# Giving out the frames of a ring in falling order of their last write

## The chip, the cores and the metric

The kernel runs on one core of one Trainium2 chip. Its time is the device time of one execution in microseconds: 972.9 us as the median of three runs (972.48 to 973.26) before the change. Five engines work side by side, each on its own queue in program order: TensorE (PE, matmuls; its weight loads are shown apart as PEld), ScalarE (ACT, activation functions), VectorE (DVE), GpSimd (POOL) and SyncE (SP, which here issues transfers). They wait for each other through semaphores.

## The reference

Attention over pooled keys, and after it a two-layer network, on 4 batches of 12,288 tokens with 128 channels:

```python
kv_pool = kv.reshape(B, H // r, r, W // r, r, C).mean(axis=(2, 4))   # r = 4
k = v = kv_pool.reshape(B, -1, C) @ w_sr                             # 768 keys a batch
a = softmax(q @ k.T / sqrt(C))
x = (a @ v).reshape(B * S, D)                                        # 49,152 tokens
h = x @ w_in                                                         # 128 -> 2048
out = (h * sigmoid(1.702 * h)) @ w_out                               # 2048 -> 128
```

## The kernel before, in words

**Tiling.** Tokens go in 96 groups of 512 (`G`, `NG`). A *chunk* is 128 x 512 values after an activation function: for attention, the exponentials of the scores of one group against 128 of the 768 keys (six chunks a group, `JC`); for the network ("MoE" in the names), the gated values of one group in 128 of the 2,048 hidden channels (16 chunks a group, `FCH`). The work goes in two rounds (`R`): attention of half of the tokens, then the network of that half, and the same again.

**Steps.** `seq` lists 700 units of up to three chunks (`K`). `fill(p)` puts up the matmuls of unit p into three PSUM banks, banks 0 to 2 and 3 to 5 in turn (`fill_attn`, L329, and `fill_moe`, L508), and one activation that turns the three banks into three chunks of bf16 in `ag` (Exp at L331, the sigmoid form of Gelu at L510). I number fills and activations from 0. A *drain* is what PE does with finished chunks: `drain_attn` multiplies 128-token pieces of attention chunks with the values (18 matmuls of 129 columns for three tiles, L340), `drain_moe` multiplies one chunk with the second weights and adds up in a bank (one matmul of 512 columns, L515). VectorE takes the sums out of banks 6 and 7 (L349 and L357 for attention, L523 for the network).

**The ring.** `ag` has 102 places for chunks (`AG`). `slot_of` holds which place each living chunk has, and a drain that used a chunk for the last time takes it out. `place` gives a unit of fill its places: the chunks of the first eight groups lie at fixed places, all others at `head`, which runs through the places in turn and begins again at `low`. `room_ahead` counts the free places from `head` on, up to the first that is taken.

**Early weights.** Four groups of the second round (`early`) have their exponentials made by VectorE during the first round's network, from a score matmul of one chunk (`early_fill`, L377; the polynomial in `early_exp`). They lie in the first 24 places: at group 12 of the network, `background_moe` sets `low` to 24, so that the ring shrinks to 78 places, and the planner sets it back to 0 when the drains of `todo_early` are done.

**The planner.** The order of all engines is written out by the program itself, while it is built, with no scheduler behind it. The loop at the end goes over the units: after `fill(n + 2)` it gives out drains and extra work (transposes, keys and values of later batches, early scores) for as long as, by the planner's own costs, the next fill is still in time for ACT (`limit`). The room in the ring enters there: extra work is put off when `room` is under four units, and a drain is given out even past the limit when `room` is under 2 K + 1, or under 4 K and the drain could start at once. What changes `room_ahead` therefore can change the order on PE and, through it, on VectorE.

**Waits.** The framework adds the semaphore waits from what each instruction reads and writes. An activation waits for PE (its fill), and, where its places were written by an earlier activation, for ACT's own semaphore too, unless ACT has already waited for that value or a later one. An instruction holds one wait; a second is an instruction of its own (EVENT_SEMAPHORE) ahead of it on the queue. In the program before, 654 such instructions stand on ACT's queue.

Of the kernel before, what the change touches and what calls it, by code (L numbers as in the profile page):

```python
# [24 lines left out]
def kernel(  # L25
# [8 lines left out]
    JC = J // 128  # L34
# [3 lines left out]
    G = 512  # L38
# [5 lines left out]
    K = 3  # L44
    T = 128
# [15 lines left out]
    EARLY = 4  # L61
    AG = 102
# [29 lines left out]
    def next_acc():  # L92
        return min((m for m in (13 - last_acc, last_acc) if m not in closes), key=lambda m: free[m])
# [67 lines left out]
    def add_kv(b, n):  # L161
        i, w = divmod(n, r)
        if n == 0:
            kv_sums[b] = kvsum.tile([Hp, 2, Wp, C], F32, name="kvs")
        for i2 in range(2):
            nc.gpsimd.dma_start(out=kv_sums[b][:, i2], in_=kv_p[b, i, w, :, i2],  # L166
                                **({"accum_op": ADD} if n else {}))
# [109 lines left out]
    ag = agpool.tile([128, AG, 512], BF, name="ag")  # L277
# [11 lines left out]


    slot_of = {}
    head, low = 8 * JC, 0

    def place(chunks):
        nonlocal head
        if chunks[0][0] == "a" and chunks[0][1] < 8:

            lo = [i * JC + jc for _, i, jc in chunks]
            slot_of.update(zip(chunks, lo))
            return ag[:, lo[0]:lo[-1] + 1:JC, :]  # L300
        if head + len(chunks) > AG:
            head = low
        lo = head
        head += len(chunks)
        busy = set(slot_of.values())
        for c in chunks:
            assert lo not in busy
            slot_of[c] = lo
            lo += 1
        return ag[:, head - len(chunks):head, :]  # L310

    def room_ahead():
        busy = set(slot_of.values())
        return next((n for n in range(AG - low) if (head - low + n) % (AG - low) + low in busy), AG - low)

    early = range(NG // R, NG // R + EARLY)

# [123 lines left out]
    def gate():  # L441

        nc.vector.memset(gate_tile, 0.0)  # L443
        nc.gpsimd.memset(gate_tile, 0.0)  # L444
# [3 lines left out]
    def background(i):  # L448

        s = i // 4  # L450
        if i % 4 == 0:
            if QS <= s + 2 < NS:
                load_qT(s + 2)
            if CAST <= s + CAST < NS:
                gate()
                cast_q(s + CAST)
        if i == 10:
            gate()
            for jc in range(JC):
                load_chunk(1, jc)  # L460
        if 0 <= i - 16 < JC:
            extras.append((key_and_value, 1, i - 16))
        if 0 <= i - 15 < JC:
            extras.append((pool_chunk, 1, i - 15))
        if i == 26:
            gate()
            nc.gpsimd.dma_start(out=w_in_sb, in_=moe_w_in)
        if i == 34:
            gate()
            nc.gpsimd.dma_start(out=w_out_sb, in_=moe_w_out.rearrange("(o p) c -> p o c", p=128))  # L470

    def background_moe(g):

        n, g = divmod(g, 4 * XS)
        m, odd = divmod(g - 9, 2)
        if n == 0 and 0 <= m < (RT - LATER[0]) // PART:
            (bring_back if odd else put_away)(n, m)
        g += n * 4 * XS
        nonlocal head, low
        if g == 12:  # L480
            low = EARLY * JC
            head = max(head, low)
        if g in (40, 46):
            i = early[0] + 4 * (g // 46)
            begun.add(("a", i))
            background(i)
        for b, lo in ((2, 2), (3, 24)):
            if lo <= g < lo + 8:
                gate()
                add_kv(b, g - lo)  # L490
            if g in (lo + 10, lo + 12):
                use_kv(b, (g - lo - 10) // 2)

    def use_kv(b, a):
        nonlocal extra_at
        sum_kv(b, a)
        on_dve(3.5)
        extra_at = max(extra_at, dve + 1.5)
        extras.extend([(transpose_pooled, b, a), (make_k, b, a), (make_v, b, a)])
# [31 lines left out]
    chunks, sizes = [], [1, 3, 3, 1, 3, 1, 3, 1] + [3, 3, 2] * 4  # L531
# [5 lines left out]
    todo_early = [("a", t, a) for t in range(NT) for a in range(2) if (t // TS * TS + TS - 1) // 4 in early]  # L537
# [68 lines left out]
    PAUSE = 4.0  # L606
    now, end, extra_at = 0.0, [], 0.0
    source, dve = None, 0.0

    def on_dve(cost):  # L610
        nonlocal dve
        dve = max(dve, now + 1.0) + cost


    def fill(p):
        nonlocal now
        if p >= len(seq):
            return
        kind, part = seq[p]
        prepare(p)  # L620
        lo = K * (p % 2)
        (fill_attn if kind == "a" else fill_moe)(part, banks[:, lo:lo + len(part), :])
        if p >= 2:
            now = max(now, end[p - 2] + HANDOVER / 2)
        now += len(part)
        begin = max(now + HANDOVER / 2, end[p - 1] if p else 0.0)
        if p and kind != seq[p - 1][0]:
            begin += SWITCH
        end.append(begin + FIXED + CHUNK * len(part))
# [3 lines left out]
    for n in range(len(seq)):  # L633
        fill(n + 2)
        while True:
            room = room_ahead()
            limit = end[-1] - K - HANDOVER if n + 3 < len(seq) else 1e9
            bank = free[next_acc()]
            f = None
            if turns and max(now, bank) >= turns[0][0]:  # L640
                f, args = turn, turns[0][1:]
            if f is None and extras and now >= max(extra_at, bank):
                f, *args = extras[0]
            if steps and dve <= now + 2.0:
                early_step()
            if not f and not steps and early_todo and low and min(slot_of.values()) >= low and (2, 1) in vs and dve <= now + 2.0 and now >= bank:
                f, args = early_fill, early_todo[0]
            if f and max(now, bank) + COST[f][0] > limit + (LATE if f is turn else 0.0 if f is early_fill else 4.5) and room >= 4 * K:
                f = None
            if f:  # L650
                now = max(now, bank) + COST[f][0]
                f(*args)
                free[last_acc] = dve + 1.0 if f is early_fill else now + COST[f][1]
                if f in (transpose_pooled, make_k, make_v):
                    on_dve(2.5)
                extra_at = max(now + PAUSE, dve + 1.5 if f in (transpose_pooled, make_k, make_v) else 0.0)
                if f is turn:
                    turns.pop(0)
                elif f is early_fill:
                    pass  # L660
                else:
                    extras.pop(0)
                continue
            if not source:

                if todo_early and all((i, jc) in made for t in range(todo_early[0][1], todo_early[0][1] + TS)
                                      for i in [t // 4] for jc in range(JC)):
                    source = todo_early
                else:
                    source = todo  # L670
            if not source:
                break
            kind, i, c = source[0]
            needs = at[("at" if kind == "a" else kind, i, c)]
            cost = K * SMALL if kind == "a" else 1.0
            first_of = c == 0 and (kind == "m" or i % TS == 0)
            if source is not todo_early and (needs > n or (kind == "a" and first_of and at["at", i + TS - 1, 1] > n)
                                             or (kind == "a" and i // 4 in early and (i // 4, JC - 1) not in made)):
                if first_of:
                    source = None  # L680
                break
            start = now if source is todo_early else max(now, end[needs] + HANDOVER)
            if first_of:
                start = max(start, bank)
            if start + cost > limit and not (room < 2 * K + 1 or (room < 4 * K and start == now)):
                if first_of:
                    source = None
                break
            now = start + cost
            (drain_attn if kind == "a" else drain_moe)(i, c)  # L690
            source.pop(0)
            if not todo_early:
                low = 0
            if c == (1 if kind == "a" else FCH - 1) and (kind == "m" or i % TS == TS - 1):
                source = None
    assert not todo and not todo_early and not turns and not extras and not early_todo
# [30 lines left out]
```

## Time and profile before

| | before |
|---|---|
| time | 972.9 us (972.48 to 973.26) |
| span of the profiled run | 971.3 us |
| PE busy | 946.9 us (97%), 6,245 matmuls recorded |
| ACT busy | 946.5 us (97%), 705 instructions |
| DVE busy | 345.0 us (36%) |
| PE weight loads busy | 505.1 us (52%) |
| TensorE clock | 0.999 of full speed |

How to read it: the first round's attention runs to about 150 us, its network to 499 us, the second attention to 619 us, and the second network to the end. PE and ACT are both busy nearly all of the time, so the busy shares can't tell which of them the other waits for; a matmul's record reaches to the modelled end of its pass through the array, and so overlaps the next one's. The start-to-start time of neighbours tells more: 216 ns for matmuls of 512 columns, 57 ns for those of 129, and from end to end 1,343 ns for activations of 1,536 values that follow each other without a wait.

### The profile page before, as it was taken

How to read it: one execution, taken by the hardware profiler on the slowest of the kernel's cores; microseconds unless marked ns; L12 is line 12 of the kernel's file. 1: busy time of each engine (PE TensorE's matmuls, PEld its weight loads, DVE VectorE, ACT ScalarE, POOL GpSimd, SP SyncE). 2: the span in 40 equal slices, each digit the busy share in tenths (PEclk: the TensorE clock that was granted, in tenths of full speed). 3: DMA queues.
4: the chain of work that ended last, by engine and by line, in shares of the span. 5: the costliest groups of instructions: out<-in, count | busy, mean ns of one | idle time of the engine just before them, and what ended most of it. 6: DMA issues, size and time to landing. Idle time of an engine off the chain costs nothing.

```text
span 971.3 us, 15718 instructions
## 1 busy us (share of the span) xinstructions
PE 946.9 (97%) x6245; PEld 505.1 (52%) x6359; DVE 345.0 (36%) x734; ACT 946.5 (97%) x705; POOL 65.6 (7%) x113
## 2 busy tenths in 40 slices
PE   7899999999999999999999999999999999999997
PEld 3567777544444444454445777754444444444443
DVE  4444433201578787877312333311101101001010
ACT  4999999999999999999999999999999999999997
POOL 3100100340000232000000000000000000000000
PEclk9999999999999999999999999999999999999999
DMA  9898751899862799224338985652222222222222
GB/s 180 159 198 156 104 101 34 104 148 163 169 133 33 106 148 115 40 36 79 59 62 159 170 160 121 132 120 44 34 44 43 34 44 33 43 34 40 37 33 44
DMA packets 354169, 89.70 MB, mean 92 GB/s; under 512 B 328048, under 2 KB 351728, under 8 KB 353776
## 3 DMA queue, kind: packets, MB, share of 16 engines
q1 hardware_dynamic: 323936, 56.06, 33.3%
q0 software_dynamic: 29104, 32.51, 22.2%
q8 instruction: 49, 0.80, 0.3%
q10 hardware_dynamic: 1056, 0.13, 0.1%
q14 instruction: 24, 0.20, 0.1%
HBM read 52.49 MB, written 45.88 MB: 101 GB/s over the span
## 4 chain that ended last, share of the span: by engine, by line
PE 73%; ACT 20%; DMA 3%; issue 2%; DVE 1%; POOL 0%; POOLq 0%
PE banks L508 24%; PE banks L515 24%; ACT ag L510 19%; PE banks L340 13%; PE banks L329 10%; DMA qT<-q_bf 2%; ACT ag L331 1%; DMA x<-in_q_dram 1%; DVE qT L230 1%; PE banks L377 0%; PE banks L419 0%; PE banks L224 0%; DVE o_sb L523 0%; PE banks L134 0%; PE banks L177 0%
## 5 line engine op out<-in xcount | busy, mean ns | idle before, releaser
L510 ACT ACTIVATE ag<-banks 128x1536 bf16<-128x1536 f32 x512 | 690.1, 1534 | 2.2 <-PE banks L508 2.2
L508 PE MATMUL banks<-x,w_in_sb 128*128 128x512 bf16 x1507 | 412.8, 378 | 2.1
L515 PE MATMUL banks<-ag,w_out_sb 128*128 128x512 bf16 x1496 | 407.2, 379 | 2.5 <-ACT ag L510 0.5
L331 ACT ACTIVATE ag<-banks 128x1536 bf16<-128x1536 f32 (+1 forms) x188 | 250.7, 1446 | 13.2 <-PE banks L329 12.5
L515 PEld LDWEIGHTS <-w_out_sb 128*128 128x128 bf16 x1536 | 149.8, 98 | 181.9 <-issue 1.5
L508 PEld LDWEIGHTS <-w_in_sb 128*128 128x128 bf16 x1536 | 147.7, 97 | 177.3 <-issue 23.6
L523 DVE STREAM_TRANSPOSE o_sb<-banks 128x512 f32<-128x512 f32 x96 | 68.7, 716 | 401.8 <-PE banks L515 382.0
L340 PEld LDWEIGHTS <-ag 128*128 128x128 bf16 x2304 | 146.3, 98 | 45.0 <-issue 1.2
L340 PE MATMUL banks<-v,ag 128*128 128x129 bf16 x2304 | 162.5, 220 | 0.4 <-DVE v L158 0.3
L329 PE MATMUL banks<-qT,kT 128*128 128x512 bf16 x507 | 147.2, 379 | 9.7 <-ACT ag L331 4.8
L349 DVE RECIPROCAL rec<-banks 128x3 f32<-128x3 f32 x128 | 23.1, 180 | 132.5 <-PE banks L340 132.5
L404 DVE SCALAR_TENSOR_TENSOR ea<-ea,eb 128x512 f32<-128x512 f32 x96 | 66.1, 688 | 2.8
L329 PEld LDWEIGHTS <-kT 128*128 128x128 bf16 x552 | 47.4, 98 | 36.2 <-issue 4.5
L357 DVE TENSOR_TENSOR x<-banks,rec 128x384 bf16<-128x384 f32 x104 | 58.0, 558 | 3.6
L166 POOL DMA_DIRECT2D kvs<-in_kv_dram x32 | 40.3, 1309 | 15.7 <-DMA kvs<-in_kv_dram 11.9
L444 POOL MEMSET gate_tile<- 1x8 f32 x38 | 4.0, 106 | 462.1 <-DVE gate_tile L443 462.1
L393 DVE TENSOR_SCALAR ea<-banks 128x512 f32<-128x512 f32 x24 | 16.6, 692 | 28.0 <-PE banks L377 28.0
L406 DVE SCALAR_TENSOR_TENSOR ag<-ea,ee 128x512 bf16<-128x512 f32 x24 | 16.5, 690 | 1.2
L399 DVE SCALAR_TENSOR_TENSOR eb<-eb,ea 128x512 f32<-128x512 f32 x24 | 16.5, 689 | 0.7
L357 DVE TENSOR_TENSOR xt<-banks,rec 128x384 bf16<-128x384 f32 x24 | 13.4, 558 | 0.8
L230 DVE COPY qT<-banks 128x512 bf16<-128x512 bf16 x15 | 9.8, 687 | 5.3 <-PE banks L224 5.2
L401 DVE TENSOR_SCALAR ea<-eb 128x512 f32<-128x512 f32 x24 | 11.0, 456 | 0.7
(65 smaller groups left out, 150.8 us busy)
## 6 DMA issues: line engine op xcount, KB each, us to landing
out_dram<-o_sb SPq DMA_DIRECT2D x382, 64.0 KB, 2.0
kvs<-in_kv_dram POOLq DMA_DIRECT2D x32, 384.0 KB, 6.4
q_bf<-in_q_dram POOLq DMA_DIRECT2D x20, 512.0 KB, 7.8
x_bf<-x SPq DMA_DIRECT2D x13, 768.0 KB, 5.7
x<-in_kv_dram POOLq DMA_DIRECT2D x12, 512.0 KB, 12.7
x<-in_q_dram POOLq DMA_DIRECT2D x3, 512.0 KB, 20.0
w_in_sb<-in_moe_w_in_dram POOLq DMA_DIRECT2D x1, 512.0 KB, 5.2
w_out_sb<-in_moe_w_out_dram POOLq DMA_DIRECT2D x1, 512.0 KB, 7.0
```

Source lines behind the costliest of these rows:

```text
L166: nc.gpsimd.dma_start(out=kv_sums[b][:, i2], in_=kv_p[b, i, w, :, i2], **({"accum_op": ADD} if n else {}))
L230: nc.vector.tensor_copy(dst, src)
L329: nc.tensor.matmul(ps[:, k, :], kTs[i // GB][:, jc * 128:(jc + 1) * 128], rhs, start=True, stop=True)
L331: nc.scalar.activation(place([("a",) + c for c in chunks]), ps, AF.Exp, scale=scale)
L340: nc.tensor.matmul(av_of[u][:, k * (C + 1):(k + 1) * (C + 1)], weights(("a", i, jc))[:, o:o + T], vs[i // GB][:, jc, 0:C + 1], start=(jc = ...
L349: nc.vector.reciprocal(rec, ps[:, :, C])
L357: nc.vector.tensor_tensor(to, ps[:, :, 0:C], rec.unsqueeze(2).broadcast_to([128, TS, C]), MUL)
L404: nc.vector.scalar_tensor_tensor(a, a, COEFFS[k], b, ADD, MUL)
L508: nc.tensor.matmul(ps[:, k, :], w_in_sb[:, fc * 128:(fc + 1) * 128], x[:, g % (4 * XS) * G:(g % (4 * XS) + 1) * G], start=True, stop=True)
L510: nc.scalar.activation(place([("m",) + c for c in chunks]), ps, AF.Gelu_apprx_sigmoid)
L515: nc.tensor.matmul(o_of[g], w_out_sb[:, fc, :], weights(("m", g, fc)), start=(fc == 0), stop=(fc == FCH - 1))
L523: nc.vector.transpose(o_sb, o_of.pop(g))
```

## The change

The 102 places become 34 frames of three. `place` gives each unit one whole frame (the fixed places of the first eight groups stay). When its list `order` is empty, it takes all frames free at that time, sorted by the number of the unit that wrote them last, and gives them out from the youngest write to the oldest; then it makes a new list. `room_ahead` counts three places for every free frame, wherever it lies. The first 24 places are taken out of the list at group 12 as before, and come back when the last drain of the early groups themselves is given out (`early_left`), no longer when `todo_early` is empty.

It is meant for ACT's queue: once ACT has waited for the youngest write of a list, the other frames of the list need no wait on its own semaphore any more.

```diff
     slot_of = {}
-    head, low = 8 * JC, 0
+    low = 0
+    written = [0] * (AG // K)
+    order, unit = [], 0
+
+    def free_frames():
+        busy = {s // K for s in slot_of.values()}
+        return [f for f in range(low // K, AG // K) if f not in busy]
 
     def place(chunks):
-        nonlocal head
+        nonlocal order, unit
+        unit += 1
         if chunks[0][0] == "a" and chunks[0][1] < 8:
             lo = [i * JC + jc for _, i, jc in chunks]
-            slot_of.update(zip(chunks, lo))
-            return ag[:, lo[0]:lo[-1] + 1:JC, :]
-        if head + len(chunks) > AG:
-            head = low
-        lo = head
-        head += len(chunks)
...
+            step = JC
+        else:
+            if not order:
+                order = sorted(free_frames(), key=lambda f: written[f])
+            f = order.pop()
+            lo = range(f * K, f * K + len(chunks))
+            step = 1
+        for c, s in zip(chunks, lo):
+            assert s not in slot_of.values()
+            slot_of[c] = s
+            written[s // K] = unit
+        return ag[:, lo[0]:lo[-1] + 1:step, :]
 
     def room_ahead():
-        busy = set(slot_of.values())
-        return next((n for n in range(AG - low) if (head - low + n) % (AG - low) + low in busy), AG - low)
+        return K * len(free_frames())
...
         if g == 12:
             low = EARLY * JC
-            head = max(head, low)
+            order[:] = [f for f in order if f >= low // K]
...
+    early_left = 2 * (G // T) * EARLY
...
-            if not todo_early:
-                low = 0
+            if kind == "a" and i // 4 in early:
+                early_left -= 1
+                if not early_left:
+                    low = 0
```

More of the change, by code (lines that the diff above doesn't have):

```diff
@@ L291 @@
     slot_of = {}
-    head, low = 8 * JC, 0
+    low = 0
[4 more added lines that the diff above has]
+        return [f for f in range(low // K, AG // K) if f not in busy]
     def place(chunks):
-        nonlocal head
+        nonlocal order, unit
+        unit += 1
         if chunks[0][0] == "a" and chunks[0][1] < 8:
             lo = [i * JC + jc for _, i, jc in chunks]
-            slot_of.update(zip(chunks, lo))
-            return ag[:, lo[0]:lo[-1] + 1:JC, :]
-        if head + len(chunks) > AG:
-            head = low
-        lo = head
-        head += len(chunks)
-        busy = set(slot_of.values())
[L306 to L310, printed above, removed]
+            step = JC
[10 more added lines that the diff above has]
+        return ag[:, lo[0]:lo[-1] + 1:step, :]
     def room_ahead():
-        busy = set(slot_of.values())
-        return next((n for n in range(AG - low) if (head - low + n) % (AG - low) + low in busy), AG - low)
+        return K * len(free_frames())
     early = range(NG // R, NG // R + EARLY)
@@ L478, in background_moe @@
         g += n * 4 * XS
-        nonlocal head, low
+        nonlocal low
         if g == 12:
             low = EARLY * JC
-            head = max(head, low)
+            order[:] = [f for f in order if f >= low // K]
         if g in (40, 46):
```

## The prediction

> **What bounds the kernel now.** I read the page's chain and costliest groups first, then the chain for stretches of the span, then the waits of TensorE's weight loads, then single hand-offs in the timeline.
>
> The page says that ACT and PE are both 97% busy; the chain says which of them gates.
>
> ```profile
> PE 73%; ACT 20%; DMA 3%; issue 2%; DVE 1%; POOL 0%; POOLq 0%
> ...
> L510 ACT ACTIVATE ag<-banks 128x1536 bf16<-128x1536 f32 x512 | 690.1, 1534 | 2.2 <-PE banks L508 2.2
> ...
> L331 ACT ACTIVATE ag<-banks 128x1536 bf16<-128x1536 f32 (+1 forms) x188 | 250.7, 1446 | 13.2 <-PE banks L329 12.5
> ```
>
> Each of the 700 activations is one step: PE fills three banks, ACT turns them into one frame of the ring, PE drains older frames. Cut at 800 us, the chain is first PE's and then ACT's (two answers, 600 to 800 us and 800 to 965 us):
>
> ```profile
> by line: PE banks L508 43.3%; PE banks L515 42.1%; PE banks L340 9.9%; PE banks L329 4.1%; issue 0.6%
> ```
> ```profile
> by line: ACT ag L510 94.0%; issue 4.6%; PE banks L515 0.9%; PE banks L508 0.8%
> ```
>
> Who waits shows in the second weight load of a fill: it sits idle where PE has to wait until ACT has left the banks (total us, times, longest; 375 to 480 us, then 800 to 965 us). There are no such waits from 90 to 150 or from 480 to 800 us.
>
> ```profile
> PEld L508 <- issue: 2.1, 11, 0.2
> ```
> ```profile
> PEld L508 <- issue: 20.2, 119, 0.2
> ```
>
> So from 100 to 800 us PE runs without a break but for 22 places, where its matmuls slip 1.73 us in all by start times; only from 803 us on does it wait 52 ns in every step. In those last 165 us ACT ends one activation every 1343 ns whatever its waits.
>
> The instruction whose number the change cuts is the extra wait on ACT's queue (lines L331 and L510):
>
> ```profile
> L331 ACTq EVENT_SEMAPHORE  x138: 17/17/17, 63.6 to 617.8; - x138
> ```
> ```profile
> L510 ACTq EVENT_SEMAPHORE  x512: 17/17/17, 149.7 to 963.6; - x171
> ```
>
> Its price at a hand-off where ACT is starved: with one wait, and with two.
>
> ```profile
> 79.57 0.81 PE L329 MATMUL banks<-qT,kT 128*128 128x512 bf16 x3
> ```
> ```profile
> 80.42 1.45 ACT L331 ACTIVATE ag<-banks 128x1536 bf16<-128x1536 f32 x1
> ```
> ```profile
> 417.79 2.20 PE L340 MATMUL banks<-v,ag 128*128 128x129 bf16 x36
> ...
> 419.83 0.81 PE L508 MATMUL banks<-x,w_in_sb 128*128 128x512 bf16 x2
> ...
> 420.47 1.46 PE L515 MATMUL banks<-ag,w_out_sb 128*128 128x512 bf16 x6
> ...
> 420.73 1.45 ACT L510 ACTIVATE ag<-banks 128x1536 bf16<-128x1536 f32 x1 [1.24 <-PE banks L508]
> ...
> 422.68 1.45 ACT L510 ACTIVATE ag<-banks 128x1536 bf16<-128x1536 f32 x1 [0.49 <-PE banks L508]
> ```
>
> The first fill ends at 80.38 and ACT starts at 80.42: 36 ns in the trace's nanoseconds, at every starved start with one wait. The second ends at 420.64, ACT starts at 420.73: 97 ns. The second wait costs 61 ns, and only there. The same lines show the kernel's largest stall: 36 attention drains in one step, then six MoE drains in the next.
>
> **What the Trainium skill says.** "Perfetto Trace Analysis", Identifying Dependency Chains: an instruction that waits on several engines may have EventSemaphore instructions put before it; the 650 rows above agree. It gives no price, so I use 61 ns. "TensorE: Matmul & The Clock Gate", Back-to-back issue gap: N/2.4 + 2.5 ns, so 216 ns for 512 columns and 56 for 129; the trace has 216 and 57. "ScalarE: Activation LUTs", What ACT_TABLE_LOAD costs: 186 ns + 0.833 ns per element with immediates, neighbours overlapping by 93, so 1466 and 1373 ns; the trace has 1450 and 1343, which I use.
>
> **The change part by part.**
>
> *Extra waits: 650 down to about 70 (the built program's order).* A frame taken from the top of the falling list carries the youngest write of the list, so the wait for it covers the rest of the list. Where ACT is fed in time, the extra wait is processed while the previous activation runs, and its removal is worth nothing: that covers the 119 steps after 803 us. Where ACT is starved, PE has no break, and an activation that starts 61 ns earlier does not move the next matmul. It pays once where a PE-bound stretch passes into one in which PE waits for ACT: there PE's wait of about 52 to 60 ns shrinks. Six such stretches follow a starved start (at 88, 310, 387, 427, 462 and 803 us): at most 6 x 61 = 0.37 us, at least none. The writes are safe as before: an activation waits for its fill, which stands on PE behind all drains that freed the frame, so no new wait on PE arises. The self-waits left are for activations at least three back, long ended.
>
> *Order of PE.* Room is now counted in whole free frames. The counts of matmuls do not change; their places do: PE's order is the same through the first 177 fills (255 us), and then drains move by one step here and there. I price a step as 3 x 0.216 for its fill, 0.216 per MoE drain or early score, 0.0567 per attention drain (36 in 2.04 us), less 1.343: what is over is taken from PE's lead, what is left ACT loses. Three MoE drains give -0.05, four +0.17. The largest lead follows from before's step 335 (18 attention and 2 MoE drains, +0.76): 0.547 us were lost at 471.7, behind steps of +0.17, -0.05, -0.05, so the lead can be 0.76 + 0.07 - 0.55 = 0.28; with one wait less, 0.34.
> - Before, fills 298 to 305: 36 attention drains (+1.34), six MoE drains (+0.60), a five-drain step: ACT lost 0.12 + 1.34 + 0.60 + 0.10 = 2.17 us.
> - After, the same stretch: three drains each at 298 and 299; the 36 stand as 18 + one early score at step 303 (+0.54) and 18 + five MoE drains at 304 (+1.40). Lead before it: 0.34, less 0.17 of a four-drain step, plus 0.05 twice at most = 0.20. Lost: 0.34 + 1.40 = 1.74. Gain 0.43.
> - Step 335: before 0.55 lost; after, three MoE drains there: 0. Gain 0.54. The moved 18 come as 12 and 6 + three MoE drains at steps 345 and 346 behind two four-drain steps: lead 0.14 against +0.29, so 0.15 lost.
> - Steps 177 to 297: early scores and two groups of attention drains change places. The same walk gives 0.13 lost, less 0.11 from the hand-offs = 0.02 lost net. From 350 on, equal work in other steps: 0.01 gained.
> - Fill 54 (87.6 us) and the first PE-bound stretch: 0.05 + 0.06 gained.
>
> Sum: 0.43 + 0.54 - 0.15 - 0.02 + 0.01 + 0.11 = 0.92 us. The same walk over before's order gives each of its five large losses within 20 ns and the end within 0.5 us, and of the sum 0.3 us is the wait and 0.6 the order. 972.9 - 0.9 = 972.0.
>
> *What the trace of before does not show:* whether the moved early scores (L377) wait for VectorE to free a bank. Before, one of 24 waited, 165 ns; behind it on PE stand the next drains and fills. From below 0, from above 24 x 0.165 = 4.0 us; I take none, as VectorE is 36% busy. The changed time at which the 24 frames of early weights come back (before about fill 348, now about 356) is nothing: the walk has it in the order. Python's bookkeeping runs at build time.
>
> **The rivals.**
> - *Every starved hand-off pays.* 30 starts with two waits lost over 50 ns between 87 and 800 us: 30 x 61 = 1.8 us, and 0.6 of order: 970.5. For it: ACT is visibly idle there. Against: PE is unbroken around nearly all of them, so its work, not the hand-off, sets the pace.
> - *The order gives nothing.* PE's work is the same in sum, and the losses only change places: 0.3 of waits alone: 972.6. For it: the clump of 36 stays. Against: step 335's loss has no equal later.
> - *Slower.* The moved early scores and the 36 drains, now beside an early score, find banks that VectorE has not freed: half the bound is 2.0 us: 972.0 + 2.0 = 974.0. For it: no view of before can exclude it. Against: 23 of 24 did not wait.
>
> **How the numbers follow.** Forecast 0.62, every hand-off 0.11, order gives nothing 0.20, slower 0.07. The time is the forecast's, 972.0. The range 971.2 to 973.2 holds the first and third, with the 0.4 us by which the runs of before lie apart from their median; it leaves out the second and most of the fourth. Faster by over 0.2% is below 970.95: the 0.11. Slower by over 0.2% is above 974.85: the upper part of the fourth, 0.04. Even removing all of PE's 1.73 us of waits and the hand-off at 803 us would only reach 971.1. Within: 0.85.
>
> **What would show it.** Right: about 70 extra waits on ACT's queue; starved starts 36 ns behind the fill; ACT still one per 1343 ns after 800 us; the idle before L510 at 415 to 423 us replaced by one of about 1.7 us near 425 us; none at 471. Wrong: a DVE releaser before L377 or L340; a PE that waits in every step well before 800 us (ACT would gate more than I think); activations that last longer than 1343 ns from end to end.

## The result, and the profile after

| | before | after |
|---|---|---|
| time, first comparison | 972.69 us (972.24 to 973.26) | 971.51 us (971.32 to 972.16) |
| ratio, 95% interval | | 0.9989 (0.9971 to 1.0006) |
| the same kernel in a later comparison | 972.57 us | 971.55 us, ratio 0.9991 (0.9983 to 0.9999) |
| span of the profiled run | 971.3 us | 969.7 us |

The change gains about 1 us, 0.1%; the first comparison alone does not tell it from none, the second just does. The forecast was 0.9 us. Neither interval tells this from the rival "the order gives nothing" (0.3 us, a ratio of 0.9997); the count below does.

The page's chain and costliest groups of the kernel after:

```profile
ACT 48%; PE 47%; DMA 3%; DVE 1%; issue 1%; POOL 0%; POOLq 0%
...
L515 ACT ACTIVATE ag<-banks 128x1536 bf16<-128x1536 f32 x512 | 690.0, 1543 | 1.6 <-PE banks L513 1.5
...
L336 ACT ACTIVATE ag<-banks 128x1536 bf16<-128x1536 f32 (+1 forms) x188 | 250.6, 1445 | 12.2 <-PE banks L334 11.7
```

The activations are as busy as before to 0.2 us, and less idle in both groups (lines L336 and L515 here are L331 and L510 of the kernel before). The chain looks like another kernel's, ACT 48% where it was 20%; the experiments show that this is not to be believed. The extra waits on ACT's queue went from 650 rows to 66:

```profile
L336 ACTq EVENT_SEMAPHORE  x16: 17/17/17, 63.1 to 613.4; - x16
```
```profile
L515 ACTq EVENT_SEMAPHORE  x50: 17/17/17, 148.9 to 932.5; - x50
```

The timeline where the prediction put the remaining clump (start us, us, instruction):

```profile
423.43 0.84 PE L345 MATMUL banks<-v,ag 128*128 128x129 bf16 x12
...
424.11 0.38 PE L382 MATMUL banks<-qT,kT 128*128 128x512 bf16 x1
...
424.32 0.50 PE L345 MATMUL banks<-v,ag 128*128 128x129 bf16 x6
...
424.66 0.81 PE L513 MATMUL banks<-x,w_in_sb 128*128 128x512 bf16 x2
...
425.31 1.18 PE L345 MATMUL banks<-v,ag 128*128 128x129 bf16 x18
...
425.51 1.45 ACT L515 ACTIVATE ag<-banks 128x1536 bf16<-128x1536 f32 x1 [0.23 <-PE banks L513]
...
426.33 1.24 PE L520 MATMUL banks<-ag,w_out_sb 128*128 128x512 bf16 x5
...
427.41 0.81 PE L513 MATMUL banks<-x,w_in_sb 128*128 128x512 bf16 x3
...
428.25 4.15 ACT L515 ACTIVATE ag<-banks 128x1536 bf16<-128x1536 f32 x3 [1.30 <-PE banks L513]
```

18 drains and a score delay the fill at 424.66, 18 and five the one at 427.41. The first of these fills ends at 425.47, and ACT starts 36 ns later. Counted from end to end of neighbouring activations, with 1,343 ns taken off, ACT lost 0.34 and 1.40 us here and 0.17 near 485 us; the walk of the prediction (its sum over TensorE's order, step by step) had 0.34, 1.40 and 0.15.

This count is the measure of the rest of the document. It takes the time from the end of one activation to the end of the next, less the 1,343 ns of an activation that follows without a wait; what is over is what ACT *lost* there. The table sums it, in us, by number of the activation, the three loads of function tables (1.42 us each) left out. The first 52 activations lose between 9.4 and 10.6 us, differently from run to run of one kernel too; most of the difference lies at the second activation, which waits for the first inputs. So the medians scatter by half a microsecond where this count does not. Each ratio is to the runs of before in the same comparison.

| kernel | 52-179 | 180-297 | 298-356 | 357-444 | 445-699 | sum | against before | median, us | ratio to before (95%) |
|---|---|---|---|---|---|---|---|---|---|
| before | 1.36 | 0.22 | 2.73 | 1.01 | 0.81 | 6.13 | | 972.5 | |
| after | 1.27 | 0.26 | 1.93 | 0.91 | 0.91 | 5.28 | -0.85 | 971.51 | 0.9989 (0.9971 to 1.0006) |
| e1 | 1.27 | 0.16 | 2.65 | 0.93 | 0.87 | 5.88 | -0.25 | 972.20 | 0.9998 (0.9990 to 1.0006) |
| e2 | 1.31 | 0.36 | 2.05 | 0.88 | 1.12 | 5.72 | -0.41 | 972.13 | 0.9996 (0.9988 to 1.0004) |
| e3 | 1.27 | 0.26 | 1.93 | 0.00 | 0.00 | 3.46 | -2.67 | 969.81 | 0.9972 (0.9960 to 0.9983) |
| e4 | 1.27 | 0.39 | 0.44 | 5.44 | 1.15 | 8.69 | +2.56 | 975.07 | 1.0033 (1.0021 to 1.0046) |
| e5 | 1.27 | 0.16 | 2.65 | 0.93 | 0.85 | 5.86 | -0.27 | 972.05 | 0.9995 (0.9987 to 1.0004) |
| e6 | 1.27 | 0.39 | 0.44 | 0.89 | 1.15 | 4.14 | -1.99 | 970.56 | 0.9981 (0.9974 to 0.9987) |
| e7 | 1.27 | 0.39 | 0.44 | 0.00 | 0.00 | 2.10 | -4.03 | 969.17 | 0.9967 (0.9955 to 0.9980) |
| e8 | 1.27 | 0.44 | 0.97 | 0.00 | 0.00 | 2.68 | -3.45 | 969.23 | 0.9969 (0.9957 to 0.9982) |
| e9 | 1.31 | 0.50 | 1.03 | 0.12 | 0.23 | 3.19 | -2.94 | 969.43 | 0.9969 (0.9957 to 0.9981) |
| e10 | 0.46 | 0.81 | 2.33 | 0.18 | 0.00 | 3.78 | -2.35 | 970.18 | 0.9976 (0.9968 to 0.9984) |
| e11 | 1.27 | 0.26 | 1.93 | 0.91 | 0.91 | 5.28 | -0.85 | 971.55 | 0.9991 (0.9983 to 0.9999) |

### The profile page after: what moved, and what is told of

Same layout as the page of the kernel before. It is cut to its first block, busy times and chain, and to the rows that moved or that the text cites. A ratio compares the mean times of both kernels' runs of the same rounds, so it can differ in the third digit from the quotient of the medians.

```text
span 969.7 us, 15127 instructions
## 1 busy us (share of the span) xinstructions
PE 946.0 (98%) x6244; PEld 504.7 (52%) x6359; DVE 344.0 (35%) x734; ACT 946.4 (98%) x705; POOL 65.7 (7%) x113
## 4 chain that ended last, share of the span: by engine, by line
ACT 48%; PE 47%; DMA 3%; DVE 1%; issue 1%; POOL 0%; POOLq 0%
ACT ag L515 36%; PE banks L513 17%; PE banks L520 17%; ACT ag L336 13%; PE banks L345 6%; PE banks L334 5%; DMA qT<-q_bf 2%; DMA x<-in_q_dram 1%; DVE qT L230 1%; PE banks L382 1%; PE banks L424 0%; PE banks L224 0%; DVE o_sb L528 0%; ACT L515 0%; PE banks L134 0%
## 5 line engine op out<-in xcount | busy, mean ns | idle before, releaser
L515 ACT ACTIVATE ag<-banks 128x1536 bf16<-128x1536 f32 x512 | 690.0, 1543 | 1.6 <-PE banks L513 1.5
L336 ACT ACTIVATE ag<-banks 128x1536 bf16<-128x1536 f32 (+1 forms) x188 | 250.6, 1445 | 12.2 <-PE banks L334 11.7
L528 DVE STREAM_TRANSPOSE o_sb<-banks 128x512 f32<-128x512 f32 x96 | 68.7, 716 | 398.8 <-PE banks L520 386.5
L426 DVE COPY x<-banks 128x768 bf16<-128x768 bf16 x12 | 6.7, 557 | 12.0 <-PE banks L424 11.9
```

The costliest lines, as they stand in the source:

```text
L336: nc.scalar.activation(place([("a",) + c for c in chunks]), ps, AF.Exp, scale=scale)
L515: nc.scalar.activation(place([("m",) + c for c in chunks]), ps, AF.Gelu_apprx_sigmoid)
L528: nc.vector.transpose(o_sb, o_of.pop(g))
```

## The experiments

**The waits without the order (e1, e5), the order without the waits (e2).** The programs as built show first that the prediction had the wrong cause for the new order. The ring of before, its places given out by falling frames but its room still counted from `head` on, builds to TensorE's order of the changed kernel, step for step. The changed kernel with a rising list builds to the order of before, step for step. So the way in which room is counted moves nothing. What moves is the start of the early scores, which waits until no living chunk lies in the first 24 places: the falling list leaves one there a little longer, the first score goes from behind fill 177 to behind fill 180, and the rest follows. To take waits and order apart, e1 and e5 therefore keep the ring of before for the planner (the early scores too begin by this ring) and give the chunks other frames. In e2 the rising list brings the waits back, and `n >= 178` holds the early scores until fill 180 (`n` runs two behind the fill); its order is that of the changed kernel but for one early score that stands one drain earlier.

```diff
 e1, e5: the ring of before for the plan, falling frames for the chunks
...
+            order = sorted(free_frames(), key=lambda f: written[f])
+        f = order.pop()
...
+            place_of[c] = f * K + k
...
-        return ag[:, slot_of[c], :]
+        return ag[:, place_of[c], :]
 e2: the change, with
-                order = sorted(free_frames(), key=lambda f: written[f])
+                order = sorted(free_frames(), key=lambda f: -written[f])
-            if not f and not steps and early_todo and low and min(slot_of.values()) >= low and ...
+            if not f and not steps and early_todo and low and min(slot_of.values()) >= low and n >= 178 and ...
```

> TensorE's order is that of the kernel before, step for step; only the frames are given out in falling order, which leaves 69 extra waits on ScalarE's queue in place of 654. Theory A (TensorE sets the pace to 800 us, so the 61 ns pay only where it goes over into waiting): 0.3 to 0.4 us faster than before, 972.3; the losses at 415 to 423 us stay at 1.34 and 0.60, that at 471 us falls from 0.55 to 0.48; starved starts 36 ns behind their fill. Rival B (every starved start pays): 30 x 61 ns, 1.8 us faster, 970.9. Rival C (all is the order): no change.

In e1 the 24 early places come back one unit of drains too soon, so that the last early tile reads weights that are partly overwritten; the work is the same. e5 holds them for the time that is needed.

> As e1_few_waits (TensorE's order of the kernel before, frames in falling order, 73 extra waits), but the 24 frames of early weights come back only when the last early drain is given out. Theory A: as e1, 0.3 us faster than before; ScalarE's losses near 420 us 1.40 and 0.54, near 471 us 0.48. Rival B (every starved start pays 61 ns): 1.8 us.

> TensorE's order is that of the changed kernel, step for step; the list is given out in rising order, which brings back 651 extra waits. Theory A: 0.54 us faster than before, 972.1; losses of 0.40 and 1.40 near 425 us and 0.21 near 485 us, none at 471 us; starved starts 97 ns behind their fill. Rival B: 0.6 us slower than A says or no gain at all. Rival C: the whole 0.9 us, 971.8.

Waits alone: -0.25 and -0.27 us by the count, where theory A had 0.3 to 0.4 and rival B 1.8. The losses at 420 and 422 us are 1.40 and 0.54 us in e1 and e5; their sum is that of before (1.34 + 0.60), and the one at 471 us is 0.49 for 0.55. Order alone: -0.41 us, where 0.54 was expected. Here 0.30 us is lost at one place, 784.2 us, that has nothing to do with the order (last section); the stretch around it, 445 to 699, loses 0.21 more than in the changed kernel. Without these 0.21 us, order and waits add up to 0.87 to 0.89, and the change has 0.85. The times of the three kernels do not differ from that of before beyond their intervals, but they put B out: 1.8 us would be a ratio of 0.9981. Some 30 starved starts with the short hand-off gain a quarter of a microsecond, since TensorE does not come any sooner.

The same kernels settle the chain. Section 4 of the page of e5 (order of before, few waits), and of e2 (order after, many waits):

```profile
ACT 84%; PE 11%; DMA 3%; DVE 1%; issue 1%; POOL 0%; ACTq 0%; POOLq 0%
```
```profile
PE 81%; ACT 13%; DMA 3%; issue 1%; DVE 1%; POOL 0%; ACTq 0%; POOLq 0%
```

TensorE's order of e5 is that of before, its losses are within 0.3 us of it, and its time within 0.05%; yet the chain goes through ACT for 84% instead of 20%. Two engines that are both full leave the chain two ways back at each step, and here the extra wait decides which it takes. My first view in the prediction leaned on it; the waits of the weight loads carried the conclusion.

**TensorE in time (e3).** From fill 359 on the planner counts the same work 1% dearer.

```diff
+    def slow(p):
+        return 1.01 if p > 358 else 1.0
-        now += len(part)
+        now += len(part) * slow(p)
-            cost = K * SMALL if kind == "a" else 1.0
+            cost = (K * SMALL if kind == "a" else 1.0) * slow(n + 2)
```

> The changed kernel, but from fill 359 on the planner counts TensorE's work 1% dearer, so that it gives out fewer drains a step and leaves them for the last 165 us, where TensorE waits 52 ns in every step. The same work in all. Theory A (TensorE late by its own load): ScalarE's losses between 510 and 800 us (1.5 us beside the table loads) go to none, TensorE waits in every step from about 690 us; 1.5 us faster than the changed kernel, 970.0 or 2.4 faster than before. Rival B (the hand-off makes those losses): they stay, since the waits are the same; no change from the changed kernel.

Measured: 2.67 us less lost than before, 1.8 less than after, all of it after activation 356, where nothing is lost any more. The waits of the weight loads from 800 to 965 us, in the kernel after and in e3:

```profile
PEld L513 <- issue: 18.2, 107, 0.2
```
```profile
PEld L513 <- issue: 6.8, 40, 0.2
```

The drains that came too early before now fill the breaks that TensorE had in the tail. (They spread further than I thought: from 600 to 800 us only 5 such waits stand in e3, not one in every step.) Its waits and hand-offs are those of the changed kernel, so this separates A from B from the other side: the losses came from TensorE's load. The planner's costs fit this: it takes a step of three fill matmuls and twelve attention drains for 3 + 12 x 0.26 = 6.12 of its units and an activation for 6.255, which is 1,343 ns; the trace has 3 x 216 + 12 x 56.7 = 1,328 ns, which is 6.19 units. TensorE is 1% slower than planned, and the plan gives out drains until ACT's time is used up (`limit`), so nothing is left for that 1%.

**The start of the early scores (e4, e6).**

```diff
 e4: the change, with
+ ... min(slot_of.values()) >= low and n >= 200 and ...
 e6: e4, with
-    opool = ctx.enter_context(tc.tile_pool(name="op", bufs=3))
+    opool = ctx.enter_context(tc.tile_pool(name="op", bufs=4))
-                    xt_of[u // 2] = npool.tile([128, 2 * TS, C], BF, name="xt")
+                    xt_of[u // 2] = npool.tile([128, 2 * TS, C], BF, name="xt", bufs=2)
```

> The changed kernel, but the early scores begin 22 steps later (not before step 200). Counts, waits and frames as in the changed kernel; only the order moves. Theory A, with the order as its larger part: the 36 attention drains no longer come in two steps that follow each other; losses of 0.23 and 0.12 are left of 1.75 and 0.15; 1.4 us faster than the changed kernel, 2.3 faster than before, 970.4. Rival C2 (the falling frames or the way in which room is counted matter, the start of the early scores does not): no change from the changed kernel.

Half right. Activations 298 to 356 lose 0.44 us where they lost 1.93, near to what the walk gave. But 4.5 us are lost in one place that the walk can't see, for it knows no VectorE. ACT, TensorE and VectorE of e4 around it:

```profile
512.81 1.45 ACT L336 ACTIVATE ag<-banks 128x1536 bf16<-128x1536 f32 x1 [3.42 <-PE banks L334]
515.11 1.45 ACT L336 ACTIVATE ag<-banks 128x1536 bf16<-128x1536 f32 x1 [0.84 <-PE banks L334]
```
```profile
507.83 0.45 PE L345 MATMUL banks<-v,ag 128*128 128x129 bf16 x5
510.98 0.51 PE L345 MATMUL banks<-v,ag 128*128 128x129 bf16 x4 [2.71 <-DVE gate_tile L448]
```
```profile
501.02 0.43 DVE L402 TENSOR_SCALAR ee<-eb 128x512 int32<-128x512 f32 x1
505.55 0.72 DVE L528 STREAM_TRANSPOSE o_sb<-banks 128x512 f32<-128x512 f32 x1 [4.10 <-DMA out_dram<-o_sb]
...
510.24 0.69 DVE L411 SCALAR_TENSOR_TENSOR ag<-ea,ee 128x512 bf16<-128x512 f32 x1
```

VectorE stands 4.10 us before L528 until a transfer of an output buffer has landed. Behind it in its queue is the rest of an early polynomial, whose last step writes `ag` at 510.24 to 510.93; the drain that reads it starts at 510.98. (The row names `gate_tile`, the next thing that VectorE ended: the last semaphore event, not the one that was needed.) In the changed kernel the last early weights are written 5.0 us before their drains begin (476.71 and 481.70 us); with the start 22 steps later nothing of this is left.

> As e4_late_start, but four output buffers for VectorE instead of three (and two of the buffers xt instead of three, to make room). Theory D (in e4 VectorE stood 4.1 us behind a transfer of an output buffer, so that the last early weights came too late for their drain on TensorE): the loss of 4.48 us near 513 us is gone, 970.3, 2.2 us faster than before. Rival E (an early start so late leaves VectorE too little time whatever the buffers): at least 2 us of it stay, 973 or more.

Measured 1.99 us less lost than before, and no loss at 513 us; TensorE's order as built is that of e4, step for step. With a fourth buffer the same transpose waits for no transfer:

```profile
502.08 0.71 DVE L528 STREAM_TRANSPOSE o_sb<-banks 128x512 f32<-128x512 f32 x1
```

Theory D stands.

**The parts together (e7, e8), and with the waits back (e9).** e7 is e6 with the plan of e3. e8 is e3 with `n >= 190`, three output buffers as in the change. e9 is e8 with the rising list.

> e6_late_four_out and the dearer plan of e3 together. Theory A with D: the gains add up, as they lie in different stretches: 1.4 by the later start and 1.5 by the plan on top of the changed kernel's 0.9, 4.0 us faster than before, 968.5. Rival: as e6's rival, 971 or more.

> The changed kernel with the dearer plan of e3 and the early scores from step 190 on, three output buffers as before. Theory A: one loss of 0.50 us near 447 us in place of 1.75 and 0.17; 3.5 us faster than before, 969.0. If the early weights again come too late near the change of stage (theory D for a start 10 steps earlier): a loss of some us near 500 us, 971 or more.

> e8_start_190 with the list given out in rising order, TensorE's order step for step as in e8, and some 650 extra waits on ScalarE's queue again. Theory A: the waits cost 0.2 us here, as TensorE is then mostly in time: 3.4 us faster than before, 969.1. Rival B (each starved start pays, or ScalarE's queue as such): 1 us or more slower than e8.

By the count e7 gains 4.03 us and e8 3.45, as expected; their medians say 3.4 and 3.3 us, with half-widths of over 1 us. Both beat the changed kernel. e9 has some 580 waits more than e8 (651 for 68 as built) and TensorE's order of e8. It loses 0.5 us more by the count, of it 0.36 at three late starts of the last section; the medians, 0.2 apart, do not tell the two. By the count the waits that the change removes cost 0.5 us here, where 0.2 was expected.

**Putting off more (e10), and the changed kernel again (e11).** In e10 `slow` gives 1.006 instead of 1.0 up to fill 358.

> e8_start_190 with TensorE's work counted 0.6% dearer before fill 359 too. Theory A, with the full ring: what is put off from the first round's attention has to be done while the ring is full, so 0.6 us less lost before 255 us, and 1.9 us more lost from 300 to 500 us (1.15 and 0.60 near 440 us, 0.48 near 490 us): 2.2 us faster than before, 970.2, 1.3 slower than e8. Rival (putting off drains always pays): 0.6 us faster than e8, 968.6.

> The changed kernel once more, beside e9 and e10 on one chip. Theory A: 0.9 us faster than before, 971.5; the losses of 0.34, 1.40 and 0.17 us at their places again, the time of the first activations apart, which hangs on the first loads.

e10: 0.81 us less lost up to activation 179, 1.7 more from 180 to 356, 0.2 later: 1.1 slower than e8 by the count, 0.95 by the medians. From step 274 to the second attention the planner of e10 counts at most nine free places, so drains are due at once. What was put off until then stands there in one piece, 36 attention drains in one step and six of the network in the next (PE and ACT of e10, where ACT starved behind them):

```profile
438.08 2.20 PE L345 MATMUL banks<-v,ag 128*128 128x129 bf16 x36
...
440.77 1.46 PE L520 MATMUL banks<-ag,w_out_sb 128*128 128x512 bf16 x6
```
```profile
440.97 1.45 ACT L515 ACTIVATE ag<-banks 128x1536 bf16<-128x1536 f32 x1 [1.02 <-PE banks L513]
442.91 1.45 ACT L515 ACTIVATE ag<-banks 128x1536 bf16<-128x1536 f32 x1 [0.49 <-PE banks L513]
```

So putting off paid in e3, where a later break took the work, and not here. e11 repeats the changed kernel: the same losses to 10 ns, and a median within 0.05 us.

## Why the prediction was right

- *TensorE sets the pace to 800 us.* Right. Shown by e3, which moves only TensorE's work and takes away what was lost there, and by e5, where shorter hand-offs do not. The chain shown first in the prediction was no evidence for it.
- *61 ns a wait, and only at the change from PE-bound to waiting.* Right in price (36 and 97 ns in every kernel, but for the late starts of the last section) and in size: I had 0.3 to 0.4 us, the count has 0.25 to 0.27.
- *The order of PE.* Right in the losses, each within 20 ns: 0.34 + 1.40 and 0.17. The lead before step 303 is written wrong: 0.34 - 0.17 + 2 x 0.05 is 0.27, not 0.20, and the order as built has only one three-drain step there, which makes it 0.22; the loss of 0.34 us measured behind a step of +0.54 means 0.20. Wrong in the cause: "Room is now counted in whole free frames" moved nothing; the later start of the early scores did, as the built programs show.
- *Steps 177 to 297 and from 350 on.* I had 0.02 lost and 0.01 gained net; the count has 0.04 lost up to 297, and 0.1 gained against 0.1 lost after 356.
- *The bound from above for the early scores.* Taken at none, and it was none in the changed kernel. That it is not free in general e4 shows: the wait that I feared came at the drain of the early weights, and cost 4.5 us.
- *The sum.* 0.92 forecast, 0.85 by the count. The profiled spans differ by 1.6 us; the other 0.8 lie in the first 52 activations, whose loss differs as much between e1 and e5, with nearly the same waits. That the median of the first comparison came out 1.2 us lower is in part this scatter, and no merit of the forecast.
- *The bound of 971.1 us for all of TensorE's waits and the hand-off at 803 us.* Wrong as a limit, though the changed kernel stays above it. It left TensorE's work in its steps; this work can be put off into the breaks after 803 us, and e3, which does only this to the changed kernel, reaches 969.81 us.
- *The matmul price.* In the Trainium skill, "TensorE: Matmul & The Clock Gate", Back-to-back issue gap, the formula that gives 216 ns stands for a matmul by itself; for a stream with weight loads the page states about 131 ns at 512 columns. The streams of this trace, each matmul with a weight load of its own, take 216 ns, so the measurement decides.

## What to carry to other kernels

When two engines are both full, do not ask the chain which of them sets the pace. Take the one that should end an instruction at fixed intervals (here ACT), count what it loses from end to end, and look for the engine that has no break at those places: a wait removed on the other is worth only the few places where the pace changes hands. The price of a wait can be read at a starved start; what its removal gains can't. And where an order is planned ahead, a change of buffers can act through the plan: compare the built orders before giving a gain to the instructions that were removed.

## What the runs showed of the hardware that was not expected

In four kernels some activations began late although their fill had long ended and TensorE was busy. Ten of them cost ACT more than 60 ns: three before (0.32 us at 87.6, 0.10 at 522.9, 0.21 at 609.8), three in e2 (0.30 at 784.2 the largest), three in e9 (0.17 at 695.6 the largest) and one in e10, which has few waits (0.18 at 533.8). The place in e2:

```profile
782.97 0.81 PE L513 MATMUL banks<-x,w_in_sb 128*128 128x512 bf16 x3
...
784.16 1.45 ACT L515 ACTIVATE ag<-banks 128x1536 bf16<-128x1536 f32 x1 [0.19 <-ACT ag L515]
```

And in e10:

```profile
532.59 0.81 PE L334 MATMUL banks<-qT,kT 128*128 128x512 bf16 x3
```
```profile
533.77 1.45 ACT L336 ACTIVATE ag<-banks 128x1536 bf16<-128x1536 f32 x1
```

In e2 the fill ends at 783.78 and the activation starts 0.38 us later, in e10 at 533.40 and 0.37 us later. All ten start 373 to 396 ns behind their fill, where 36 or 97 is the rule, and all ten stand at the same kind of place. Counted along ACT's records in the trace, extra waits included, each is the 64th or a multiple of 128 further (704th and 832nd before, 704th, 960th and 1088th in e2 and e9, 448th in e10), with its extra wait just ahead. From activation 30 on, the 13 traces have 14 activations at such places with an extra wait just ahead, and none of them starts sooner than 373 ns behind its fill. Activations at the same places without an extra wait start as soon as 36 ns behind it, and 64 records away even those with an extra wait start 97 ns behind it. So a late start takes both, an extra wait and the place where it falls, and a kernel with few waits seldom has one.

The page shows transfers of instructions on a queue of their own, q14: 24 in the kernels with many waits, 19 or 20 in the others, each of 8 KB. Such a transfer follows each of the ten late starts by 0.6 to 3.8 us. That ACT takes up its instructions in pieces of 128 and is held where a wait and its activation fall into two of them would fit; no run tests it.
